# Turning normalized tokens by transfers and 32x32 blocks on VectorE in place of TensorE transposes, in a linear-attention and two-MLP kernel

## The chip, the cores and the metric

One core of one Trainium2 chip runs the whole program. Times are device microseconds of that core. The kernel before was timed three times: 986.84 to 987.23 us, median 987.09. Engines are named as in the profile: PE is TensorE's matmuls, PEld its weight loads, DVE is VectorE, ACT ScalarE, POOL GpSimd, SP the engine that issues nearly all transfers.

## The reference

```python
def phi(x):                                   # x is q or k, (4, 8, 576, 64), times 64 ** -0.25
    h = einsum('bhsd,md->bhsm', x, omega) - sum(x * x, -1) / 2
    return exp(h - max(h, -1)) / sqrt(128)
num = einsum('bhsm,bhmd->bhsd', phi(q), einsum('bhsm,bhsd->bhmd', phi(k), v))
x = num / (einsum('bhsm,bhm->bhs', phi(q), sum(phi(k), 2)) + 1e-6)      # to (2304, 512)
xn = x / sqrt(mean(x * x, -1) + 1e-6) * rms_g
y = (silu(xn @ w_gate) * (xn @ w_val)) @ w_out                          # 512 -> 1536 -> 512
out = silu(y @ w_in) @ w_out2                                           # 512 -> 2048 -> 512
```

Everything is float32 but the weights of the two MLPs, which come in as 64-bit words and are turned into float32 pairs on the chip.

## The kernel before

The 2304 tokens are 18 tiles of 128: 16 main tiles (a batch, a half, one of two interleaved rows) and 2 tail tiles of two batches each. Four tiles make a block; the normalized tokens of block j lie feature-first in the SBUF tile xs[j], which the instruction order names xs_90 to xs_94 (xs_93 is block 3, the last four main tiles; xs_94 the two tail tiles). Each float32 operand of a large product is kept as a high and a low part, and a product is three passes of TensorE.

The program has two phases.

**Phase one, 0 to 192.4 us**, is attention, normalization, the preparation of the first weights and the first gate, value and output products of blocks 0 to 2. It is a list of small operations (class `Op`: engine, estimated length, what it waits for, buffers claimed and freed) that `run_order` emits in the order of the hand-written table `ORDER`; each engine works its own part of that table strictly in order, SP's transfers too. Products of blocks 0 to 2 (line 248, line 1037) stand between attention pieces in the table.

A token tile passes through these steps: numerators on TensorE (line 813); denominators, reciprocal and quotient on VectorE (lines 827, 830, 840) into `xt`; the square sum on ScalarE (`square`, line 878); the power -1/2 on GpSimd (`rstd`, lines 889 and 892); the scale on ScalarE (`scale_x`, line 908, in place in `xt`); then `flip_x` (line 917), four 128x128 transposes on TensorE into a PSUM buffer `b`; `x_hi` on ScalarE (line 926) and `x_lo` on VectorE (line 931) read that PSUM buffer and write the high and low part of xs[j]. `xt` has two buffers, each for the two tiles of a half batch, freed by the last flip; `b` has six.

```python
        def flip_x(o):
            st.pt = buf(ps_a, [P, KC, P], "b", o.slot["b"])
            for c in range(KC):
                nc.tensor.transpose(st.pt[:, c, :], st.x[:, c * P:(c + 1) * P], ident)
```

Other names in the rows: line 658 is the feature projection, line 788 the flip of the exponentials e (evacuated to qT at line 794), line 729 the kv product, lines 154 to 192 the decoding of weight words (raw, m) into high and low parts (w). Gate and value weights are loaded by line 144, one transfer of 128x4x256 words each, other weights by line 142; `rms_g` by line 1114 into g_sb.

**Phase two**, from 192.43 us, is `stream()`: the first sweep on blocks 3 and 4 (`g1_glu`, tiles g, line 248), then all further sweeps of both MLPs, with weight preparation between (`Prep.tick`).

## Time and profile before

| what | value |
|---|---|
| median of three runs | 987.09 us (986.84 to 987.23) |
| profiled execution, own time | 987.54 us |
| its span, first to last instruction | 985.8 us |
| granted TensorE clock, mean | 1.00 of full speed |
| busy us: PE, DVE, ACT, POOL | 979.3 (99%), 562.8 (57%), 400.9 (41%), 294.2 (30%) |
| start of the stream | 192.43 us |

The span is a little shorter than the execution's own time, since it runs from the first to the last instruction. Busy shares over the whole span average two phases of a different kind; the stages are read apart below. In the chain of waits a piece is what the end of the program hung on at that moment.

### The profile page before, as it was taken

The numbers are of one execution on the slowest core, as the hardware profiler recorded it, in microseconds if no ns is written. First come the engines' busy times: TensorE is split into PE (matmuls) and PEld (weight loads), VectorE is DVE, ScalarE is ACT, GpSimd is POOL, SyncE is SP. The second block draws the span as 40 slices with busy tenths as digits, with TensorE's granted clock in tenths as the row PEclk, the third lists the DMA queues.
The fourth block names the chain that finished last, engine by engine and source line by source line (L and its number), as shares of the span: only waits on it lengthen the run. The fifth ranks groups of instructions, "written<-read, shape, count | busy, mean of one in ns | idle before, by whom it ended". The sixth has DMA issues, their size and how long they took to land.

```text
span 985.8 us, 15373 instructions
## 1 busy us (share of the span) xinstructions
PE 979.3 (99%) x6010; PEld 835.4 (85%) x6010; DVE 562.8 (57%) x1168; ACT 400.9 (41%) x922; POOL 294.2 (30%) x308
## 2 busy tenths in 40 slices
PE   9999999999999999999999999999999999999998
PEld 8999988887888888888898888888888888888887
DVE  7998976668633265774234773614634634535633
ACT  6999977753311123341112334443222223222321
POOL 8888664245400022442001322402402312201200
PEclk9999999999999999999999999999999999999999
DMA  7646220123200012221000121201101201100023
GB/s 182 156 115 164 80 63 22 44 65 101 71 21 0 1 43 65 83 89 44 1 1 5 60 65 43 64 22 44 64 22 40 68 22 44 43 1 22 22 86 107
DMA packets 69112, 55.58 MB, mean 56 GB/s; under 512 B 26160, under 2 KB 63280, under 8 KB 69040
## 3 DMA queue, kind: packets, MB, share of 16 engines
q1 hardware_dynamic: 68768, 54.54, 19.0%
q8 instruction: 47, 0.77, 0.3%
q14 instruction: 25, 0.20, 0.1%
q10 hardware_dynamic: 272, 0.07, 0.0%
HBM read 49.87 MB, written 4.72 MB: 55 GB/s over the span
## 4 chain that ended last, share of the span: by engine, by line
PE 94%; DVE 2%; DMA 1%; ACT 1%; issue 0%; POOL 0%; SPq 0%; DVEq 0%
PE g L248 45%; PE y L335 20%; PE y L302 13%; PE b L658 5%; PE b L248 3%; PE b L813 2%; PE kv L729 2%; PE b L1037 2%; PE b L788 2%; PE b L629 2%; PE b L917 1%; DVE w L192 1%; DMA va<-in_v_dram 1%; DVE small L675 0%; DMA raw<-in_moe_w_out_dram 0%
## 5 line engine op out<-in xcount | busy, mean ns | idle before, releaser
L248 PE MATMUL g<-xs,w 128*128 128x512 f32 (+1 forms) x2256 | 469.4, 367 | 0.0
L248 PEld LDWEIGHTS g<-xs,w 128*128 128x128 f32 x2256 | 391.2, 188 | 71.7
L168 POOL TENSOR_TENSOR m<-m,raw 128x512 int32<-128x512 int32 x136 | 189.5, 1393 | 590.6 <-issue 422.3
L242 DVE TENSOR_TENSOR h<-s,h 128x512 fp32r<-128x512 f32 (+1 forms) x134 | 95.8, 715 | 186.2 <-ACT h L241 186.2
L335 PE MATMUL y<-w,h 128*128 128x512 f32 (+1 forms) x870 | 201.0, 388 | 0.0
L335 PEld LDWEIGHTS y<-w,h 128*128 128x128 f32 x870 | 162.2, 188 | 33.3
L241 ACT ACTIVATE h<-s 128x512 fp32r<-128x512 f32 (+1 forms) x134 | 78.7, 588 | 184.2 <-DVE s L271 162.2
L302 PE MATMUL y<-h,w 128*128 128x512 f32 (+1 forms) x648 | 135.6, 366 | 0.5 <-DVE w L192 0.5
L302 PEld LDWEIGHTS y<-h,w 128*128 128x128 f32 x648 | 112.1, 189 | 20.8 <-DVE w L192 0.9
L282 ACT ACTIVATE s<-g 128x512 f32<-128x512 f32 (+1 forms) x80 | 44.5, 556 | 172.1 <-PE g L248 166.9
L346 DVE TENSOR_TENSOR ya<-y,ya 128x512 f32<-128x512 f32 (+1 forms) x91 | 62.2, 684 | 58.0 <-PE y L335 56.7
L271 DVE TENSOR_TENSOR s<-s,g 128x512 f32<-128x512 f32 (+1 forms) x54 | 33.9, 627 | 85.6 <-PE g L248 83.2
L313 DVE TENSOR_TENSOR ya<-y,ya 128x512 f32<-128x512 f32 (+1 forms) x80 | 50.2, 635 | 54.1 <-PE y L302 53.9
L700 ACT ACTIVATE e<-b,nb 128x128 f32<-128x128 f32 x272 | 76.2, 427 | 3.3 <-DVE nb L688 3.1
L189 ACT ACTIVATE w<-m 128x512 fp32r<-128x512 f32 x68 | 43.1, 634 | 68.6 <-POOL m L168 68.1
L658 PE MATMUL b<-bd,hl 128*128 128x256 f32 x432 | 62.3, 289 | 0.6 <-DVE hl L646 0.5
L658 PEld LDWEIGHTS b<-bd,hl 128*128 128x128 f32 x432 | 54.2, 189 | 2.4 <-DVE hl L646 0.7
L192 DVE TENSOR_TENSOR w<-m,w 128x512 fp32r<-128x512 f32 x68 | 54.1, 795 | 2.2 <-ACT w L189 2.2
L675 DVE TENSOR_REDUCE small<-b 128x4 f32<-128x512 f32 x72 | 50.1, 695 | 8.7 <-PE b L658 6.1
L265 ACT ACTIVATE s<-g 128x512 f32<-128x512 f32 (+1 forms) x54 | 29.6, 548 | 58.2 <-PE g L248 58.1
L582 POOL TENSOR_TENSOR sq<-sq 128x256 f32<-128x256 f32 (+1 forms) x80 | 46.5, 589 | 3.2
L578 POOL TENSOR_TENSOR sq<-x 128x512 f32<-128x512 f32 (+1 forms) x40 | 39.5, 992 | 21.8 <-DVE ns L591 13.3
(72 smaller groups left out, 738.0 us busy)
## 6 DMA issues: line engine op xcount, KB each, us to landing
raw<-in_moe_w_out_dram SPq DMA_DIRECT2D x28, 512.0 KB, 3.5
raw<-in_moe_w_in_dram SPq DMA_DIRECT2D x16, 512.0 KB, 3.7
raw<-in_moe_w_gate_dram SPq DMA_DIRECT2D x12, 512.0 KB, 3.5
raw<-in_moe_w_val_dram SPq DMA_DIRECT2D x12, 512.0 KB, 3.5
x<-in_k_dram SPq DMA_DIRECT2D x16, 256.0 KB, 3.6
va<-in_v_dram SPq DMA_DIRECT2D x32, 128.0 KB, 4.2
x<-in_q_dram SPq DMA_DIRECT2D x16, 256.0 KB, 3.2
out_dram<-ya SPq DMA_DIRECT2D x15, 256.0 KB, 2.0
```

The source lines that it names most:

```text
L168: tt(out=mi, in0=mi, in1=(low if step == 5 else high).bitcast(I32), op=ALU.add)
L192: nc.vector.tensor_tensor(out=st.t[:, 1, :], in0=st.m.bitcast(F32), in1=st.t[:, 0, :].bitcast(F32), op=ALU.subtract)
L241: nc.scalar.activation(out=ht[:, 0, :], in_=s, func=AF.Copy)
L242: nc.vector.tensor_tensor(out=ht[:, 1, :], in0=s, in1=ht[:, 0, :].bitcast(F32), op=ALU.subtract)
L248: nc.tensor.matmul(out=ps, lhsT=w[:, a, cc * P:(cc + 1) * P], rhs=xs[j][:, c, cc, :], start=(n == 0), stop=(n == 3 * KC - 1),)
L302: nc.tensor.matmul(out=ps, lhsT=wt[1, "o", f][:, a, d * P:(d + 1) * P], rhs=hs[f][:, c, :], start=(n == 0), stop=(n == nn - 1),)
L313: nc.vector.tensor_tensor(out=y[:, d, :], in0=ps, in1=y[:, d, :], op=ALU.add)
L335: nc.tensor.matmul(out=ps, lhsT=hs[f][:, a, t * P:(t + 1) * P], rhs=wt[2, "p", f][:, c, d0:d1], start=(n == 0), stop=(n == nn - 1),)
L346: nc.vector.tensor_tensor(out=o[:, t, d0:d1], in0=ps, in1=o[:, t, d0:d1], op=ALU.add)
L658: nc.tensor.matmul(out=st.ps[r][:, 2 * j:2 * j + 2, :].rearrange("p h m -> p (h m)"), lhsT=st.hl[:, c, 2 * r + j, :], rhs=bd[:, a, :], sta ...
L675: nc.vector.tensor_reduce(out=st.mx[:, G * r:G * r + G], in_=st.ps[r], axis=AX.X, op=ALU.max)
L700: nc.scalar.activation(out=st.e[r][:, h, :], in_=st.ps[r][:, h, :], func=AF.Exp, bias=st.nb[:, G * r + h:G * r + h + 1],)
```

## The change

Lines of the changed kernel are named where they matter: the numerators are line 850 there, denominators 864, quotient 877 and 884, the square 915, the power 926 and 929, the scale 945, e's flip 826 and its evacuation 832, the output product 1084, its sum 1096, the gate and value product 256, weight loads 146 and 148.

- `flip_x` becomes `move_x`: four transfers issued by SP per tile (line 954), each from 128 features of all 128 tokens in `xt` into one group of 32 partitions of xs[j], where the high part will be; the issue waits for the scale.
- A new VectorE operation (line 964) turns that 128x512 tile in blocks of 32x32 back into `xt`, writing with a step of four elements.
- `x_hi` (line 972) and `x_lo` (line 977) read the turned `xt` in SBUF instead of PSUM. `xt` is freed by the last x_lo, and the x_lo of a pair are chained. [...]
- A partition of xs[j] now holds other features than before (feature 128a + 32c + d instead of 128c + p), so the rows of gate and value weights are loaded to fit: each of the 24 loads is four transfers of 32x4x256 words. `g_sb` too is loaded in four.
- The pad EDGE lies in the third early weight tile to be allocated rather than in the one with slot 2.
- The flip of e by transfers is written in as well, but no tile uses it (`BY_DMA` is empty).
- `ORDER` is written anew (1239 operations instead of 1221).

```diff
-        def flip_x(o):
-            st.pt = buf(ps_a, [P, KC, P], "b", o.slot["b"])
-            for c in range(KC):
-                nc.tensor.transpose(st.pt[:, c, :], st.x[:, c * P:(c + 1) * P], ident)
-
-        fl = Op(
-            "xf", "PE", 0.436, flip_x, [xn, getattr(xs_, "flip", None)], ["b"],
-            [(xs_.op, "xt")] if last else [],
+        def move_x(o):
+            blocked = xs[j][:, 0, :, o0:o0 + P].bitcast(F32)
+            for a in range(4):
+                nc.sync.dma_start(
+                    out=blocked[32 * a:32 * a + 32],
+                    in_=st.x[:, P * a:P * a + P],
+                )
+
+        fl = Op("xd", "SP", 2.1, move_x, [xn, getattr(xs_, "flip", None)], xfer=1.5)
+        xs_.flip = fl
+        turned = lambda: st.x.rearrange("p (c t) -> p c t", c=KC)
+        tp = Op(
+            "xT", "DVE", 0.6,
+            lambda o: nc.vector.transpose(
+                out=st.x.rearrange("p (c t b) -> p b c t", c=KC, b=4),
+                in_=xs[j][:, 0, :, o0:o0 + P].bitcast(F32).rearrange("p b (c d) -> p b c d", c=KC),
+            ),
+            [fl],
         )
         hi = Op(
             "x_hi", "ACT", 0.52,
-            lambda o: nc.scalar.activation(out=xs[j][:, 0, :, o0:o0 + P], in_=st.pt, func=AF.Copy),
-            [fl],
+            lambda o: nc.scalar.activation(out=xs[j][:, 0, :, o0:o0 + P], in_=turned(), func=AF.Copy),
+            [tp],
         )
         xslo[ti] = Op(
-            "x_lo", "DVE", 0.6,
+            "x_lo", "DVE", 0.61,
             lambda o: nc.vector.tensor_tensor(
-                out=xs[j][:, 1, :, o0:o0 + P], in0=st.pt,
+                out=xs[j][:, 1, :, o0:o0 + P], in0=turned(),
                 in1=xs[j][:, 0, :, o0:o0 + P].bitcast(F32), op=ALU.subtract,
             ),
-            [hi], free=[(fl, "b")],
+            [hi, getattr(xs_, "low", None)], free=[(xs_.op, "xt")] if last else [], port=True,
         )
...
+        if turned:
+            return [cols[P * a:P * a + P].rearrange("(c d) f -> d c f", c=KC) for a in range(4)]
...
+        if isinstance(ap, list):
+            for a, rows in enumerate(ap):
+                nc.sync.dma_start(out=raw[32 * a:32 * a + 32].rearrange("p c f w -> p c (f w)"), in_=rows)
...
+            for a in range(4):
+                nc.sync.dma_start(
+                    out=g_sb[32 * a:32 * a + 32], in_=rms_g[P * a:P * a + P].rearrange("(c d) -> d c", c=KC)
+                )
```

**TensorE ahead of the stream.** In the kernel before, from the last matmul row of the tail's numerators (b_3484; the tail's first numerators stand just above, the last main ones 23 rows earlier) on; two more output groups and the stream's `g<-xs_93` follow after the last row shown.

```order
L813 MATMUL b_3484<-kvs_2932,qT_3482 64x65
L917 MATMUL b_3495<-ident,xt_3070 128x128 x4
L917 MATMUL b_3507<-ident,xt_3070 128x128 x4
L917 MATMUL b_3513<-ident,xt_3300 128x128 x4
L1037 MATMUL b_3522<-h_3415,w_4_2954 128x512 x3
L917 MATMUL b_3527<-ident,xt_3300 128x128 x4
L1037 MATMUL b_3542<-h_3415,w_4_2954 128x512 x3
L1037 MATMUL b_3522<-h_3504,w_5_2961 128x512 x3
L1037 MATMUL b_3542<-h_3504,w_5_2961 128x512 x3
L1037 MATMUL b_3555<-h_3415,w_4_2954 128x512 x3
L1037 MATMUL b_3555<-h_3504,w_5_2961 128x512 x3
L917 MATMUL b_3566<-ident,xt_3519 128x128 x4
```

In the change, from the last main tile's numerators (b_3450, b_3468) on; after the last row one more group of six output matmuls, the tail's 16 numerator matmuls and then `g<-xs_93` follow.

```order
L850 MATMUL b_3450<-kvs_3168,qT_3434 64x65 x8
L850 MATMUL b_3468<-kvs_3168,qT_3427 64x65 x8
L826 MATMUL b_3478<-ident,e_3463 128x128 x4
L1084 MATMUL b_3495<-h_3381,w_4_2804 128x512 x3
L1084 MATMUL b_3499<-h_3381,w_4_2804 128x512 x3
L826 MATMUL b_3503<-ident,e_3282 128x128 x4
L1084 MATMUL b_3495<-h_3483,w_5_2997 128x512 x3
L1084 MATMUL b_3499<-h_3483,w_5_2997 128x512 x3
L1084 MATMUL b_3522<-h_3381,w_4_2804 128x512 x3
L1084 MATMUL b_3527<-h_3381,w_4_2804 128x512 x3
L1084 MATMUL b_3522<-h_3483,w_5_2997 128x512 x3
```

The five turns of line 917 are gone from here, the output products stand behind the main numerators, and the tail's numerators have moved behind these.

**ScalarE ahead of the stream**, in the change, from the evacuation of e's flip for the tail (qT_3508) on; the squares of the last pair of main tiles (xt_3383) stand just above. xt_3097 is the pair before, xt_3574 the last tail tile.

```order
L832 ACTIVATE qT_3508<-b_3503 128x512
L1096 ACTIVATE ya_97<-b_3495 128x512
L945 ACTIVATE xt_3383<-xt_3383,rstd_3491 128x512
L972 ACTIVATE xs_93<-xt_3097 128x4x128 x2
L832 ACTIVATE qT_3535<-b_3478 128x512
L1096 ACTIVATE ya_97<-b_3499 128x512
L945 ACTIVATE xt_3383<-xt_3383,rstd_3491 128x512
L197 ACTIVATE w_1_3576<-m_3357 128x512
L1096 ACTIVATE ya_97<-b_3527 128x512
L915 ACTIVATE xs_94,ss_3585<-xt_3574 128x4x128
L945 ACTIVATE xt_3574<-xt_3574,rstd_3586 128x512
L972 ACTIVATE xs_93<-xt_3383 128x4x128 x2
```

x_hi of the last pair (line 972, xs_93<-xt_3383) stands behind the square and the scale of the tail tile.

**SP ahead of the stream.** Before:

```order
L144 DMA raw_2888<-in_moe_w_gate_dram 128x4x256
L519 DMA x_2904<-in_q_dram 64x4x64 x2
L144 DMA raw_2934<-in_moe_w_gate_dram 128x4x256
L144 DMA raw_3266<-in_moe_w_val_dram 128x4x256
L144 DMA raw_3610<-in_moe_w_val_dram 128x4x256
L144 DMA raw_3652<-in_moe_w_gate_dram 128x4x256
L144 DMA raw_3724<-in_moe_w_val_dram 128x4x256
```

Of the change:

```order
L146 DMA raw_3057<-in_moe_w_gate_dram 32x4x256 x4
L528 DMA x_3113<-in_q_dram 64x4x64 x2
L954 DMA xs_92<-xt_2785 32x4x128 x8
L146 DMA raw_3261<-in_moe_w_val_dram 32x4x256 x4
L954 DMA xs_93<-xt_3097 32x4x128 x8
L954 DMA xs_93<-xt_3383 32x4x128 x8
L954 DMA xs_94<-xt_3574 32x4x128 x4
L146 DMA raw_3634<-in_moe_w_val_dram 32x4x256 x4
```

The moves of four main tiles and a tail tile (20 issues) now stand between the weight loads, and value loads of phase two stand behind them.

## Rows read from the trace of the kernel before

**Rows 1.** Windows by stage: length, busy us (instructions) of PE, PEld, DVE, ACT, POOL, clock, DMA, GB/s
```profile
10.00:50.00 40.00, 39.50 (x572) 37.17 (x569) 37.15 (x107) 38.72 (x127) 34.56 (x51) 1.00 0.66 165
50.00:123.00 73.00, 72.69 (x987) 67.63 (x987) 66.03 (x185) 70.54 (x214) 54.74 (x79) 1.00 0.47 121
123.00:177.00 54.00, 54.00 (x541) 46.83 (x540) 40.93 (x114) 41.22 (x107) 27.22 (x35) 1.00 0.16 49
177.00:192.40 15.40, 15.40 (x111) 12.93 (x110) 11.14 (x23) 12.66 (x29) 5.36 (x7) 1.00 0.12 35
```

**Rows 2.** Chain of waits, in order of time to 193 us: start, us, what
```profile
17.26 0.96 PE b L658 x6
...
49.19 0.50 SPq L526
...
106.14 0.87 PE b L917 x8
...
174.45 1.08 PE b L813 x32
...
183.49 1.08 PE b L813 x32
184.57 1.46 PE b L917 x12
...
191.04 1.39 PE b L1037 x6
192.43 0.70 PE g L248 x3
```

**Rows 3.** Groups of one form, 0 to 192.4 us: busy us, mean ns | idle before
```profile
L840 DVE TENSOR_TENSOR xt<-b,rd 128x256 f32<-128x256 f32 x32 | 13.0, 418 | 0.4
...
L931 DVE TENSOR_TENSOR xs<-b,xs 128x512 fp32r<-128x512 f32 x18 | 12.0, 682 | 2.6 <-ACT xs L926 2.6
L926 ACT ACTIVATE xs<-b 128x512 fp32r<-128x512 f32 x18 | 11.0, 636 | 2.4 <-PE b L917 2.2
...
L192 DVE TENSOR_TENSOR w<-m,w 128x512 fp32r<-128x512 f32 x9 | 6.9, 766 | 1.3 <-ACT w L189 1.3
...
L830 DVE RECIPROCAL rd<-rd 128x4 f32<-128x4 f32 x36 | 5.5, 169 | 0.4
```

**Rows 4.** Groups of one form on VectorE, whole span
```profile
L157 DVE TENSOR_SCALAR raw<-raw 128x512 uint32<-128x512 uint32 x68 | 31.5, 464 | 0.0
L160 DVE TENSOR_SCALAR m<-m 128x512 f32<-128x512 f32 x68 | 29.7, 436 | 0.0
```

**Rows 5.** DMA issues of all kinds: count, KB each, us to landing
```profile
raw<-in_moe_w_val_dram SPq DMA_DIRECT2D x12, 512.0 KB, 3.5
...
out_dram<-ya SPq DMA_DIRECT2D x15, 256.0 KB, 2.0
...
x<-in_q_dram SPq DMA_DIRECT2D x8, 64.0 KB, 2.4
```

**Rows 6.** Timeline from 179 to 184 us: start, us, engine, line
```profile
179.68 0.66 ACT L878 ACTIVATE xs<-xt 128x512 fp32r<-128x512 f32 x1
...
180.81 0.22 ACT L878 ACTIVATION_READ_ACCUMULATOR xs<-xt 128x1 f32 x1
...
181.12 0.19 POOL L889 TENSOR_SCALAR ss<-ss 128x2 f32<-128x2 f32 x1 [1.08 <-ACT xs L878]
...
181.39 0.69 POOL L892 TENSOR_TENSOR rstd<-ss,mhalf 128x2 f32<-128x2 f32 x1
...
182.64 1.32 ACT L908 ACTIVATE xt<-xt,rstd 128x512 f32<-128x512 f32 x2
...
183.49 0.37 SPq L144 DMA_DIRECT2D raw<-in_moe_w_gate_dram  x1
```

**Rows 7.** Timeline from 204 to 212 us, a value load and its first reading
```profile
204.61 0.37 SPq L144 DMA_DIRECT2D raw<-in_moe_w_val_dram  x1
...
211.25 1.42 DVE L154 TENSOR_SCALAR m<-raw 128x512 uint32<-128x512 uint32 x1
```

More of the change, by code (lines that the diff above doesn't have):

```diff
@@ L115, with wcols @@
     assert f == NF2
-    wt = {}
-    def wcols(w, f):
-        return w.bitcast(U32)[:, 2 * f * P:2 * (f + 1) * P].rearrange("(c p) f -> p c f", p=P)
+    wt, early = {}, []
+    def wcols(w, f, turned=False):
+        cols = w.bitcast(U32)[:, 2 * f * P:2 * (f + 1) * P]
+        if turned:
+            return [cols[P * a:P * a + P].rearrange("(c d) f -> d c f", c=KC) for a in range(4)]
+        return cols.rearrange("(c p) f -> p c f", p=P)
     def wrows(w, f):
@@ L126, in prep_list @@
         if kind == 1:
[L127 removed]
+            gv = [e for f in fs for e in (("g", f, wcols(w_gate, f, True)), ("v", f, wcols(w_val, f, True)))]
             if si == 0:
@@ L184, in w_high @@
         t = pool.tile(
-            [P, 2 * KC * P + (EDGE if pool is pools["w"][2] and slot == W_EARLY - 1 else 0)], F32R,
+            [P, 2 * KC * P + (EDGE if pool is pools["w"][2] and len(early) == W_EARLY - 1 else 0)], F32R,
             tag=f"w{side}_{slot}", name=f"w{side}_{slot}",
         )
+        if pool is pools["w"][2]:
+            early.append(slot)
         st.t = t[:, 0:2 * KC * P].rearrange("p (a n) -> p a n", a=2)
@@ L693, in add_unit @@
         res = f"et{g}" if kind == "kt" else "e"
+        base = count[0]
+        if kind[0] == "q":
+            count[0] += R
+        moved = lambda r: kind[0] == "q" and base + r in BY_DMA
         for r in range(R):
@@ L697, in exps @@
                 pool = kp if kind == "kt" else wk
-                st.e[r] = buf(pool, [P, G, M], res, o.slot[res])
+                blocks4 = moved(r)
+                st.e[r] = buf(pool, [P, 4, G, 32] if blocks4 else [P, G, M], res, o.slot[res])
                 for h in range(G):
+                    src = st.ps[r][:, h, :]
                     nc.scalar.activation(
-                        out=st.e[r][:, h, :], in_=st.ps[r][:, h, :], func=AF.Exp,
+                        out=st.e[r][:, :, h, :] if blocks4 else st.e[r][:, h, :],
+                        in_=src.rearrange("p (a f) -> p a f", a=4) if blocks4 else src, func=AF.Exp,
                         bias=st.nb[:, G * r + h:G * r + h + 1],
@@ L711, in add_unit @@
         else:
-            evs = [add_flip_e(st, r, exs[r]) for r in range(R)]
+            evs = [add_flip_e(st, r, exs[r], moved(r)) for r in range(R)]
             num = None
@@ L780, in add_kv, with add_flip_e, move, turn @@
             add_tail(b - 1, g, 1, tst, tex, vop, [(tex, f"et{g}"), (pad, f"vt{g}")])
-    def add_flip_e(st, r, ex):
+    def add_flip_e(st, r, ex, by_dma):
         pe = {}
+        if by_dma:
+            def move(o):
+                pe[0] = buf(wk, [P, G, P], "qT", o.slot["qT"])
+                for a in range(4):
+                    nc.sync.dma_start(
+                        out=pe[0][32 * a:32 * a + 32],
+                        in_=st.e[r][:, a].rearrange("p h f -> p (h f)"),
+                    )
+            def turn(o):
+                turned = st.e[r].rearrange("p a h f -> p (a h f)").rearrange("p (h t) -> p h t", h=G)
+                nc.vector.transpose(
+                    out=turned.rearrange("p h (t b) -> p b h t", b=4),
+                    in_=pe[0].rearrange("p b (h f) -> p b h f", h=G),
+                )
+                st.e[r] = turned
+            mv = Op("ed", "SP", 2.1, move, [ex], ["qT"], xfer=1.5)
+            tp = Op("eT", "DVE", 0.6, turn, [mv], free=[(mv, "qT")])
+            return tp, (ex, "e")
         def flip(o):
@@ L815, in numerators @@
                     )
-        deps = evs + [prev, kvcopy[b, g]]
-        free = [(ev, "qT")]
+        deps = [ev for ev, _ in evs] + [prev, kvcopy[b, g]]
+        free = [evs[half_unit][1]]
         if tail:
@@ L945, in load @@
             w_load(job, st, o.slot["raw"])
-        lop = Op("ld_w", "SP", 0.5, load, gate, ["raw"], xfer=2.2)
+        lop = Op("ld_w", "SP", 2.1 if scaled(job) else 0.5, load, gate, ["raw"], xfer=2.2)
         prev = head = None
@@ L1113, with load_g @@
         bd_ops += spare
-        g_op = Op("ld_g", "SP", 0.5, lambda o: nc.sync.dma_start(out=g_sb, in_=rms_g.rearrange("(c p) -> p c", p=P)))
+        def load_g(o):
+            for a in range(4):
+                nc.sync.dma_start(
+                    out=g_sb[32 * a:32 * a + 32], in_=rms_g[P * a:P * a + P].rearrange("(c d) -> d c", c=KC)
+                )
+        g_op = Op("ld_g", "SP", 2.0, load_g)
         for u in units:
```

11 lines of the change are left out of this document (6 added, 5 removed), and 139 rows, old and new, of the table ORDER.

## The prediction

> **What bounds the kernel now.** I read the page first, whose busy times stand in the table above: TensorE is busy 99% of the span, so a change pays by what it takes off TensorE, or costs by a wait that it puts there. The windows by stage show where the change acts [rows 1]. From 10 to 192.4 us TensorE is busy 39.50 of 40, 72.69 of 73, 54.00 of 54 and 15.40 of 15.4 us. Beside it, up to 123 us, ScalarE is busy 38.72 + 70.54 = 109.3 of 113 us and VectorE 37.15 + 66.03 = 103.2: the reader is to see that three engines are nearly full there, and that after 123 us the two others have room (40.93 and 41.22 of 54). The chain of waits [rows 2] runs in TensorE pieces from 17.26 us to the stream, whose first matmul starts at 192.43 us; the turns of line 917 are in it at their full length, 0.87 us for two groups of four. The kernel's grouped instructions [rows 3] give the neighbours' prices.
>
> **What is removed.** 18 groups of four transposes leave TensorE. A group costs 0.87 / 2 = 0.44 us [rows 2], so 18 x 0.44 = 7.9 us leave a bound engine. That much is sure; what matters is what becomes of it.
>
> **What is added on VectorE.** Per token tile one turn of 128x512 from SBUF to SBUF, in 32x32 blocks. The trace has no such operation. The fast end is 0.44 us, what a one-input VectorE pass over 128x512 takes (line 160, [rows 4]); the slow end is twice an ordinary pass, 2 x 0.68 = 1.36. I take 0.68, a pass with two inputs over 128x512 (line 931, [rows 3]): of the two kinds of pass in these rows it is the one that goes slower per element, and a turn has to reorder what it reads. [...] x_lo now reads two SBUF tiles rather than PSUM; the like of that, line 192, takes 0.77 instead of 0.68 [rows 3], so 0.09 more. Per tile 0.77 us, for 18 tiles 13.9 us.
>
> From 10 to 123 us the kernel before has ten of the 18 groups (in the chain the last two of them start at 106.14 us, [rows 2]), and the new order still has the first eight turns there. TensorE's work falls by 10 x 0.44 = 4.4 us, so the stretch could shrink from 113 to 108.6. But ScalarE keeps its 109.3, and VectorE needs 103.2 + 8 x 0.77 = 109.4: both more than 108.6. So at least 0.8 us of the gain is not to be had, unless work of these two moves behind 123 us (then 0). Two engines with no idle time left will not mesh perfectly; I take **1.5 us**, with 0 and 4 as ends (4 is nearly all of the 4.4). Behind 123 us VectorE had 54 - 40.93 = 13 us idle; there the turns are covered.
>
> **What is added on the queue.** Four issues of SP per tile. One costs 0.37 us (line 144, [rows 6]) to 0.50 (line 526, [rows 2]); I take 0.44, so 1.8 us per tile. A load of 64 KB, the size of the four moves together, lands after 2.4 us, and the quickest transfer here after 2.0 [rows 5]; I take 2.2. A tile therefore passes from scaled to turned in 1.8 + 2.2 + 0.68 = 4.7 us, where TensorE needed 0.44. In the middle of the phase TensorE has other units' projections and products to do meanwhile, so this is hidden. Loads that stand behind a move on SP wait for that tile's scale; they are issued several units ahead, so I price them at nothing (if the cover fails, it shows as TensorE waiting on a DMA, inside the 4 us above).
>
> **Where the latency comes out: the start of the stream.** In the kernel before 16.9 us of TensorE work stood between the last main tile's numerators, which end at 174.45 + 1.08 = 175.53, and the stream [rows 2]. In the new order only this does: two flips of e (2 x 0.44), 24 output matmuls (4 x 1.39) and the tail's numerators (1.08) [rows 2], together 7.5 us. The stream's first group needs all four tiles of block 3, high and low part. From the end of the last main numerators the way is:
> - VectorE, two times denominator, reciprocal (0.17 each) and quotient (0.42): 1.5 us, some of it overlapped with the numerators, 1.2 [rows 3];
> - ScalarE, two squares, from 179.68 to 181.03 us: 1.3; GpSimd, rstd, from 181.12 to the end of the power at 182.08: 1.0; ScalarE, the scale of tile 0, half of 1.32: 0.7 [rows 6]. That is 4.2;
> - ScalarE then does two x_hi of the earlier tiles, one qT and one ya before it scales tile 1: 4 x 0.62 + 0.66 = 3.1, 7.3;
> - SP 1.8, landing 2.2, turn 0.7, in all 4.7: 12.0; x_hi 0.64 and x_lo 0.77 [rows 3]: 13.4;
> - seven handings-over between engines, 0.09 us each at best (as from 181.03 to 181.12, [rows 6]): 14.0 us.
>
> TensorE has 7.5 us of work for these 14.0, so **it waits 6.5 us** with nothing else in its queue (5 if landing and issue take their lower prices and one overlaps, 8.5 if the issues take 0.5 and the tail's square and scale, which stand before x_hi of these tiles on ScalarE, come last). The last tile of block 4 is later still, but it is wanted 48 matmuls x 0.23 (1.39 / 6, [rows 2]) = 11 us after the stream starts, and is covered.
>
> **Edits at nothing.** 24 gate and value loads become four issues each, 3 x 0.37 to 3 x 0.5 = 1.1 to 1.5 us later: the load issued at 204.61 lands after 3.5 us and is first read at 211.25, 3.1 us of room [rows 5, 7]. The three more issues for g_sb stand ahead of other loads near the start, 3 x 0.37 = 1.1 us; the loads of values that follow are issued well ahead of their use, and I take nothing, with 1.1 us as the other end if a first use falls due there. The weight tile moved is an address.
>
> **Sum.** -7.9 + 1.5 + 6.5 = +0.1 us. The profiled execution took 987.54 us, the median of the runs is 987.09, 0.45 less; so 987.54 + 0.1 - 0.45 = **987.2 us**: the gain on TensorE is spent at the start of the stream. A measurement of this kernel can tell 0.2%, 2.0 us, from no change.
>
> **Rivals.**
> 1. *The latency is hidden and the gain stays.* If the way to the stream takes some 10 us rather than 14 (moves that land while the next is issued, both tiles in parallel) the wait is 2.5, and with 1.0 for the middle the sum is -4.4: 982.7. With no wait at all -7.9 + 0.8: 980.0. For it: the first tile's move is in flight while the second tile is still being scaled, and the prices are taken one after the other. Against it: from the quotient to x_lo of the second tile each step hangs on the one before, and 7.5 us is all the work that TensorE has.
> 2. *VectorE becomes the bound, slower.* The turn writes its elements 16 bytes apart. If that halves the rate, a turn takes 1.36 us; the eight early ones then cost 8 x 0.68 = 5.4 us more on an engine that has no idle time left, and the last one 0.7 in the way to the stream: 987.2 + 6.1 = 993.3. It decides from 0.9 us per turn on: (0.9 - 0.68) x 9 = 2.0 us, 0.2%. Against it: a VectorE pass with 8-byte steps (line 157) takes 464 ns where the dense one (line 160) takes 436 [rows 4], 6% more; no row has 16-byte steps. [...]
> 3. *The change does less than it says.* Excluded: the instruction order has no turn of token tiles on TensorE any more.
>
> **How the numbers follow.** Forecast 0.45: with the middle at 0.8 to 3 and the wait at 5 to 7.5 the sum is -2.1 to +2.6, so 985.0 to 989.7; with the far ends of both (0 and 5, 4 and 8.5) it would be 984.2 to 991.7. Rival 1 0.29 (979.5 to 985). Rival 2 0.22 (989.5 to 994). 0.04 is left for what I don't see. The range 981.0 to 991.0 takes in the forecast, most of rival 1 and the lower part of rival 2. Faster than 985.1: rival 1 and a little of the forecast, 0.32. Slower than 989.1: rival 2, the forecast's top and the rest, 0.29. Within: 0.39.
>
> **What would show it.** Right: a wait of TensorE of 5 to 8 us in one piece ahead of the first stream matmul, released by x_lo (line 977) or x_hi; turns of 0.6 to 0.8 us; moves landing in 2.0 to 2.4 us; 0 to 4 us of short waits on VectorE or ScalarE between 50 and 123 us; a stream that starts within 2 us of 192.4. Wrong: a stream that starts near 186 (rival 1), or turns over 0.9 us and many waits on VectorE (rival 2).

## The result, and the profile after

| what | before | after |
|---|---|---|
| median of the runs (four each, same chip) | 987.16 us (986.84 to 987.52) | 996.92 us (996.45 to 996.95) |
| span of the profiled execution | 985.8 us | 995.2 us |
| start of the stream | 192.43 us | 201.3 us |
| from there to the end of the span | 793.4 us | 793.9 us |
| busy us: PE, DVE, ACT, POOL | 979.3, 562.8, 400.9, 294.2 | 977.5, 582.9, 402.1, 295.2 |

The ratio is 1.0098, with a 95% interval of 1.008 to 1.0115. The change makes the kernel slower by 9.8 us, where 0.1 us was forecast and 991.0 was the top of the range. Of the span's 9.4 us, 8.9 come before the stream starts.

The windows of after, with the stretches of [rows 1] and three more around the new start:

```profile
10.00:50.00 40.00, 38.70 (x552) 35.44 (x550) 36.88 (x102) 37.48 (x123) 34.53 (x53) 1.00 0.74 169
50.00:123.00 73.00, 70.11 (x919) 63.23 (x920) 69.14 (x187) 68.68 (x205) 54.46 (x77) 1.00 0.52 137
123.00:177.00 54.00, 51.62 (x488) 43.88 (x487) 49.56 (x115) 41.39 (x112) 26.31 (x33) 0.97 0.30 80
177.00:192.40 15.40, 15.40 (x134) 12.68 (x133) 11.15 (x28) 9.80 (x25) 6.85 (x8) 1.00 0.11 31
192.40:201.30 8.90, 3.53 (x43) 2.71 (x41) 5.98 (x14) 6.54 (x14) 1.14 (x3) 0.82 0.23 67
201.30:206.00 4.70, 4.70 (x13) 3.46 (x14) 2.32 (x3) 1.62 (x3) 0.00 (x0) 0.62 0.71 176
206.00:212.00 6.00, 6.00 (x28) 4.96 (x27) 2.46 (x6) 2.31 (x4) 0.00 (x0) 1.00 0.35 70
```

TensorE had 0.5, 0.3, 0 and 0 us idle in the first four [rows 1]; now it has 1.3, 2.9, 2.4 and 0, and 5.4 in the fifth. VectorE's busy time rose from 66.03 to 69.14 in the second window and from 40.93 to 49.56 in the third. The granted clock is below 1.00 in three windows, at 0.62 in the one after the start of the stream; it was 1.00 in all stretches before.

The waits of TensorE in after (engine, line, what it waited for: us in total, times, longest):

```profile
PE g L256 <- DMA xs<-xt: 5.4, 1, 5.4
PE b L1084 <- DVE h L1060: 1.8, 1, 1.8
PE b L850 <- DVE hl L656: 1.5, 2, 0.8
...
PE b L668 <- ACT e L716: 1.0, 2, 0.8
PE b L826 <- ACT e L716: 0.8, 2, 0.6
...
PE b L850 <- DVE s L1051: 0.5, 1, 0.5
```

In before the only waits of 0.5 us or more in phase one were 1.4 us at the very start (there still) and one of 0.5 us. The first row is the wait that was forecast; the others, of 1.8 us at most, are new and on VectorE and ScalarE.

Groups of one form of after, 0 to 201.3 us (busy us, mean ns | idle before), and the issues of the moves (count, KB, us to landing):

```profile
L964 DVE STREAM_TRANSPOSE xt<-xs 128x512 f32<-128x512 f32 x17 | 18.7, 1110 | 1.2 <-DMA xs<-xt 1.1
...
L977 DVE TENSOR_TENSOR xs<-xt,xs 128x512 fp32r<-128x512 f32 x17 | 13.9, 825 | 0.9 <-ACT xs L972 0.9
...
L160 DVE TENSOR_SCALAR m<-raw 128x512 uint32<-128x512 uint32 x9 | 7.4, 825 | 0.0
L200 DVE TENSOR_TENSOR w<-m,w 128x512 fp32r<-128x512 f32 x9 | 6.1, 682 | 0.0
L163 DVE TENSOR_SCALAR raw<-raw 128x512 uint32<-128x512 uint32 x9 | 5.9, 661 | 0.0
```

```profile
xs<-xt SPq DMA_DIRECT2D x72, 64.0 KB, 2.2
```

A turn takes 1.11 us and x_lo 0.83 [before: rows 3, line 931]. The first two decode passes of a weight tile, lines 160 and 163 now, were lines 154 and 157; the rows show them at 0.83 and 0.66 us, and before they took 0.45 and 0.49:

```profile
L157 DVE TENSOR_SCALAR raw<-raw 128x512 uint32<-128x512 uint32 x9 | 4.3, 493 | 0.0
...
L154 DVE TENSOR_SCALAR m<-raw 128x512 uint32<-128x512 uint32 x9 | 4.0, 452 | 0.0
```

**Where 9.4 us of span come from.** The flips took 7.9 us off TensorE and the wait before the stream put 5.4 on. The stream starts 201.3 - 192.43 = 8.9 later, so the rest of phase one cost 8.9 + 7.9 - 5.4 = **11.4 us**, where 1.5 was forecast. The windows of that whole stretch, before and after, part it in two:

```profile
10.00:192.43 182.43, 181.63 (x2204) 164.59 (x2202) 155.27 (x426) 163.14 (x474) 121.88 (x171) 1.00 0.39 102
10.00:201.30 191.30, 179.35 (x2128) 157.94 (x2126) 172.71 (x442) 163.90 (x474) 123.29 (x171) 0.98 0.46 116
```

TensorE is idle for 191.30 - 179.35 - 5.4 = 6.6 us outside the wait, against 0.8 before: 5.8 us are new idle time. The other 5.6 are busy time: it should have fallen to 181.63 - 7.9 = 173.7 and is 179.35 for the same matmuls. Of this the clock of 0.94 in the 27 us from 150 to 177 (shown with fix150) makes 0.06 x 27 = 1.6; the rest is spread over the phase and was not traced to its places. In phase two, nearly cancelling things add up to +0.5. The first 48 matmuls of the stream take 13.03 us in the timeline (11.06 before): 2.0 lost, at the clock of 0.62. And many pieces of later gate and value products are 0.08 us shorter; one in the chain of waits of before, and its like in after:

```profile
245.51 16.40 PE g L248 x72
```

```profile
256.47 16.32 PE g L256 x72
```

After 300 us, before had six pieces of 8.24 and six of 8.16 us for 36 such matmuls; after has eleven of 8.16 and one of 8.19. With the other lengths it is 18 or 19 pieces times 0.08, about 1.5 us gained.

### The profile page after: what moved, and what is told of

It is laid out like the page before. It is cut to its first block, busy times and chain, and to the rows that moved or that the text cites. A ratio compares the mean times of both kernels' runs of the same rounds, so it can differ in the third digit from the quotient of the medians.

```text
span 995.2 us, 15601 instructions
## 1 busy us (share of the span) xinstructions
PE 977.5 (98%) x5938; PEld 830.0 (83%) x5938; DVE 582.9 (59%) x1186; ACT 402.1 (40%) x922; POOL 295.2 (30%) x308
## 4 chain that ended last, share of the span: by engine, by line
PE 86%; DVE 7%; ACT 2%; DMA 1%; issue 1%; POOL 1%; SPq 0%; DVEq 0%; ACTq 0%; POOLq 0%
PE g L256 44%; PE y L343 20%; PE y L310 12%; PE b L256 2%; PE b L668 2%; PE b L1084 2%; DVE small L685 1%; PE b L850 1%; ACT e L716 1%; PE kv L746 1%; PE b L639 1%; PE b L826 1%; DVE w L200 1%; DVE m L160 1%; DVE raw L163 1%
## 5 line engine op out<-in xcount | busy, mean ns | idle before, releaser
L592 POOL TENSOR_TENSOR sq<-sq 128x256 f32<-128x256 f32 (+2 forms) x80 | 46.7, 595 | 2.7
```

## Experiments on the turn

Times are medians; before took 986.9 to 987.2 us beside each of them. "Stream" is the start of the first product of block 3, "40 to 70" the busy time of an engine in that stretch of 30 us. Before and after have there, with the columns of [rows 1]:

```profile
40.00:70.00 30.00, 29.86 (x467) 28.08 (x467) 28.14 (x82) 29.72 (x94) 23.59 (x41) 1.00 0.41 100
```

```profile
40.00:70.00 30.00, 26.91 (x373) 24.04 (x373) 29.50 (x78) 28.33 (x86) 22.75 (x33) 1.00 0.57 143
```

**Each turn done twice** (label twice).

```diff
-            lambda o: nc.vector.transpose(
+            lambda o: [nc.vector.transpose(
...
-            ),
+            ) for _ in range(2)],
```

> Every turn is done twice (the second gives the same result): 18 x 1.1 us more on VectorE, nothing else. Theory A (VectorE is the bound up to about 123 us and partly after): the time rises by 10 to 17 us, to 1007 to 1014. Rival C (the loads behind the moves set the pace): it rises by 2 to 5 us, mostly the one turn in the way to the stream.

Measured 1011.51 us (1009.99 to 1011.71), 14.6 more than after, for 18 x 1.11 = 20 us more of VectorE, inside theory A's 10 to 17; the stream started at 214.5. So most of what is put on VectorE in this phase comes out in the time.

**Turns left out** (noturn) and **turns written densely** (dense): in the second the elements of a turn stand side by side, and the final stores put the tokens right again.

```diff
-                out=st.x.rearrange("p (c t b) -> p b c t", c=KC, b=4),
+                out=st.x.rearrange("p (c b t) -> p b c t", c=KC, b=4),
```

```diff
-            lambda o: nc.vector.transpose(
...
+            lambda o: None,
```

> The turns on VectorE are left out (so the products run on tokens that were not turned); moves, x_hi, x_lo and all else stay. Theory A: the middle gets back nearly all of the 11.4 us that TensorE falls behind there, and one turn less stands before the stream: 985 to 989. Rival C: 1 to 3 us less than the change, 994 to 996.

> The turn writes its result densely (the tokens of a tile come out in another order, which the last stores undo); everything else stays. Theory A (the 16-byte step of the turn's output costs the second half of its 1.11 us, and VectorE is the bound between 43 and 102 us): a turn takes 0.55 to 0.70 us, some 13 turns of the middle give back 0.4 us each, the time falls by 5 to 7 us to 990 to 992. Rival B (a turn of float32 takes 1.1 us whatever the step): turn and time stay, 996 to 998. Rival C (the middle loses its time to loads that stand behind the moves on SP): the turn gets faster, the time falls by less than 2 us.

Measured 994.16 us (991.74 to 995.07) without turns: only 2.8 gained, so the turns explain the smaller part of the loss and theory A fails. The time is rival C's, but not for its reason, as the run without moves below shows. Measured 1009.04 us (1008.01 to 1010.3) with dense turns, outside all three ranges. The turn itself became what the rival of the prediction needed (group of the turn, whole span):

```profile
L971 DVE STREAM_TRANSPOSE xt<-xs 128x512 f32<-128x512 f32 x18 | 12.6, 704 | 3.9 <-DMA xs<-xt 3.8
```

0.70 us dense against 1.11 with the step of 16 bytes, and the stream started at 199.3, 2.0 earlier; but the program ended 12 us later. TensorE's last matmul ended at 989.9 and the span at 1007.6, 17.7 us behind it (3.4 in after). Whether the stores did that, a second run had to tell: **dense_plain** has the dense turn and plain stores, on top of the two edits of the run both (below).

> As the run with the two edits together, with the turn written densely (no 16-byte step), and the results stored plainly, so that the tokens of a tile stand in another order in the output. Theory: a turn takes 0.70 instead of 1.11 us; 8 early ones give back about 2 us of the middle and the last one 0.4 us: 988.0 to 989.0 us, still above the kernel before, and phase two takes 793.5 to 794 us, so that the 14 us that the run with the dense turn lost at its end belong to its stores. Rival: if the dense turn is slow in phase two for another reason than the stores, the program stays near 1003 us.

Measured 990.13 us (989.53 to 991.07), against 991.21 for both. Phase two took 792.6 us, so the loss at the end of dense belonged to its stores in permuted order. The dense turn is worth 1.1 us there, half or less of what was expected.

## Experiments on the wait before the stream

**No moves and no turns** (nomove), and **blocks 3 and 4 turned on TensorE**, at the places of their moves (pe_tail).

```diff
-            for a in range(4):
-                nc.sync.dma_start(
...
+            pass
...
-            lambda o: nc.vector.transpose(
...
+            lambda o: None,
```

> Moves and turns are left out (x_hi reads the scaled, unturned tile); x_lo, weight loads and the order stay. Theory A2 (in the middle the loss lies in the new order on VectorE and ScalarE, which are full there, not in the moves on SP): the middle stays as without turns, only the wait before the stream falls by issue and landing, from 4.6 us to about 0.5, and with it the slow matmuls behind it: 987 to 990. Rival S (the moves on SP hold up loads and so the middle): it gains 3 us and more in the middle too, 980 to 986.

```diff
+        def flip_x(o):
...
+        on_pe = j >= 3
-        fl = Op("xd", "SP", 2.1, move_x, [xn, getattr(xs_, "flip", None)], xfer=1.5)
+        fl = (
+            Op("xf", "PE", 0.436, flip_x, [xn, getattr(xs_, "flip", None)], ["b"])
+            if on_pe else Op("xd", "SP", 2.1, move_x, [xn, getattr(xs_, "flip", None)], xfer=1.5)
+        )
...
```

In this edit and in pe_all below an operation whose inputs or buffers are not there yet also stands back until they are, so the order of the table is not kept throughout.

> The tiles of blocks 3 and 4 are turned on TensorE again, at the places where their moves stood; the other tiles are moved and turned as in the change (the features of those two blocks come in an order that their weights don't have). Theory A2: six flips cost 2.6 us, the wait of 5.4 us before the stream goes, and so does the slow stretch behind it; the middle stays: 992 to 995. Rival T (the wait before the stream is not from the moves but from the chain of squares and scales): the wait stays above 3 us, 996 to 1000.

Measured 994.28 us (992.87 to 994.55) and 997.94 us (996.4 to 998.64). The waits of TensorE in the first, and in the second:

```profile
PE g L256 <- ACT xs L964: 4.6, 1, 4.6
```

```profile
PE b L980 <- ACT xt L963: 3.0, 1, 3.0
```

Without moves and turns the wait is still 4.6 us: x_hi of the last pair is queued on ScalarE behind the tail tile's square and scale. With TensorE flips it is 3.0 us, released by the scale of the tail, whose flip stands ahead of the stream in TensorE's queue there. Two ways of nearly equal length lead to the stream, and neither edit takes away both. So theory A2 fails in both runs, and rival T holds in pe_tail.

The run without moves says more. Its time is that of the run without turns (994.16), so the moves and what stands behind them on SP cost little, against rival S and rival C. And its stream starts at 197.88: with neither a move nor a turn, the rest of phase one still cost 197.88 - 192.43 + 7.9 - 4.6 = 8.8 us of the 11.4. What it keeps of the change is above all x_lo from SBUF (0.85 us instead of 0.68 per tile) and the new order.

**All tiles turned on TensorE in the new order** (pe_all, `on_pe = True` in the edit above, weights in the old layout) were to show the order alone:

> All tiles are turned on TensorE in the new order, at the places where their moves stood; no moves, no turns on VectorE, x_lo from PSUM; weights and g_sb still load in four pieces, in the old layout. Theory A2 (the new order itself loses 3 to 5 us, by VectorE operations held up in 150 to 165 us): 990 to 993. Rival V (the order is as good as the old one; moves, turns and x_lo from SBUF make the whole loss): 986 to 988.5.

It took 1017.85 us (1015.3 to 1020.2) and tells nothing of the order alone: TensorE waited in some fifteen places for qT, e and the low parts of features to be written. Likely the flips at the moves' places claim PSUM buffers that this order doesn't have free; that was not tried. So no run shows the new order by itself.

**Spare matmuls in the wait** (warm): 36 matmuls of 256 columns into an unused PSUM buffer, behind the tail's numerators.

```diff
+            if tail:
+                tails.append(1)
+            if tail and len(tails) == 4:
+                spare_ps = buf(ps_a, [P, G, D + 1], "kv", 0)
+                for _ in range(36):
+                    nc.tensor.matmul(
+                        out=spare_ps.rearrange("p g d -> p (g d)")[:, 0:G * D], lhsT=xs[2][:, 0, 0, 0:P], rhs=xs[2][:, 0, 0, 0:G * D],
+                        start=True, stop=True,
+                    )
```

> 36 matmuls of 256 columns into a PSUM buffer that is free by then stand in TensorE's queue behind the tail's numerators, where it waits for the stream's tokens; nothing else. Theory K (the first 4.7 us of the stream run at a granted clock of 0.62 because TensorE was idle before): these are granted 1.0, the time falls by 1 to 2 us, to 995 to 996. Rival (the slow stretch is hidden behind later waits): 996.5 to 997.5.

Measured 994.41 us (993.03 to 994.88), 2.5 gained, a little more than theory K's 1 to 2. The windows of warm, with the columns of [rows 1]:

```profile
195.00:201.30 6.30, 5.20 (x34) 4.42 (x34) 3.65 (x6) 2.79 (x6) 0.74 (x2) 1.00 0.27 79
195.00:206.00 11.00, 9.90 (x55) 8.31 (x55) 6.11 (x8) 5.31 (x9) 0.74 (x2) 1.00 0.49 133
```

The clock stays at 1.00 where after had 0.82 and 0.62. The wait of 5.4 us thus cost its own length and 2.0 to 2.5 us of slow matmuls behind it.

**The second scale of the last pair moved up** (both_scale, on top of both), directly behind the first on ScalarE:

```diff
-        969, 1233, 907, 1236, 902, 1111, 903, 908, 1012, 1234, 970, 1237, 904, 909, 994, 995, 996,
-        1232, 974, 1013, ...
+        969, 974, 1233, 907, 1236, 902, 1111, 903, 908, 1012, 1234, 970, 1237, 904, 909, 994, 995,
+        996, 1232, 1013, ...
```

> As in the run before, and the scale of the last pair's second tile stands directly behind that of the first on ScalarE (before: two x_hi, an evacuation of e's flip and one of an output product between them). Theory T (the way of the last pair through scale, move, turn and split sets the wait): that scale starts about 1.9 us earlier and the stream 1.0 to 1.9 us earlier, 989.0 to 989.9 us. Rival U (SP's twelve issues, 0.6 to 0.8 us each, set it): the second tile's moves are issued no earlier than SP has done the first's, so 0.3 us at most, 990.6 us.

Measured 991.48 us (991.25 to 991.74), against 991.21 for both: no gain. The scales now stand together, the second 1.8 us earlier (at 188.45 instead of 190.28), and SP's row of twelve issues for the last pair and the tail tile takes the same 9.26 us. The timeline of both_scale (in both the issues run from 188.41 on, also for 9.26 us), and below it eight issues of after that stand close together:

```profile
187.84 1.33 ACT L954 ACTIVATE xt<-xt,rstd 128x512 f32<-128x512 f32 x2
188.58 9.26 SPq L963 DMA_DIRECT2D xs<-xt  x12
...
194.61 0.72 ACT L954 ACTIVATE xt<-xt,rstd 128x512 f32<-128x512 f32 x1 [0.94 <-POOL rstd L938]
```

```profile
155.66 5.17 SPq L954 DMA_DIRECT2D xs<-xt  x8
```

An issue takes 5.17 / 8 = 0.65 us, where the prediction took 0.44. The eight of the last pair take 5.1 us in both runs; the rest of the 9.26 is SP waiting for the tail's scale (194.61) and its four issues. In both_scale the second tile's scale was done at 189.2, but its first issue came at 191.2, when SP was through with the first tile's four. So SP's issues hold the way through the moves, as rival U said; the time is 0.9 us over the one that it named.

## Experiments on the middle

**x_lo left out** (nolo), **x_hi left out** (nohi), **x_hi and turns left out** (nohi_noturn).

```diff
-            lambda o: nc.scalar.activation(out=xs[j][:, 0, :, o0:o0 + P], in_=turned(), func=AF.Copy),
+            lambda o: None,
...
-            lambda o: nc.vector.tensor_tensor(
-                out=xs[j][:, 1, :, o0:o0 + P], in0=turned(),
...
+            lambda o: None,
```

> x_lo is left out for all tiles (the low parts of the tokens are what lay there before); moves, turns and all else stay. Theory A2 (VectorE's extra load is only a few us of the loss, since ScalarE is full beside it): 993 to 996. [...]

> x_hi is left out on ScalarE (the high part is then what the move put there, unturned); moves, turns, x_lo and the order stay. Theory A3 (between 45 and 110 us ScalarE and VectorE are both full and each by itself holds the pace, so that taking from one gives little): a little more than without the turns, 990 to 994. Rival V (VectorE alone holds the pace): 995 to 997. Rival S (ScalarE alone): 987 to 990.

> x_hi and the turns are left out together. Theory A3: the middle up to 110 us gets back its 3 us and more, more than the two single gains add up to; the stall near 160 us and the wait before the stream stay: 985 to 989. Rival O (the middle's loss is set by the order of TensorE's own queue, whatever the others do): as without turns alone, 993 to 995.

Measured 992.25 us (992.07 to 994.06), 996.33 (994.94 to 996.74) and 992.36 (991.65 to 993.71): 4.7, 0.6 and 4.6 gained. The first is 0.75 us under the range of theory A2, the last lies between the two ranges named for it; the second is rival V's. Taking work off VectorE helps, off ScalarE alone hardly. But even the last kept 28.02 us of TensorE in 40 to 70, 1.8 short of before, with VectorE still busy for 28.68. Something else filled VectorE.

What it was shows in the timeline of after where the 1.8 us wait for h arises (start, us, engine, line):

```profile
158.81 3.02 POOL L174 TENSOR_TENSOR m<-m,raw 128x512 int32<-128x512 int32 x2 [3.81 <-DVE rd L864]
...
159.29 1.38 DVE L1060 TENSOR_TENSOR h<-s,h 128x512 fp32r<-128x512 f32 x1 [0.48 <-ACT h L1057]
...
160.59 1.53 DVE L160 TENSOR_SCALAR m<-raw 128x512 uint32<-128x512 uint32 x1
...
161.91 1.10 POOL L177 TENSOR_TENSOR m<-m,g_sb 128x512 f32<-128x512 f32 x1
162.04 1.52 DVE L1060 TENSOR_TENSOR h<-s,h 128x512 fp32r<-128x512 f32 x1
...
163.62 0.95 PE L1084 MATMUL b<-h,w 128*128 128x512 f32 x2 [1.82 <-DVE h L1060]
```

Three VectorE passes that take 0.67, 0.42 and 0.67 us at their shortest (lines 1060 and 160) take 1.38, 1.53 and 1.52 while GpSimd adds words for a weight tile and multiplies it by g_sb (line 177). The second and the third end 0.3 and 0.55 us behind the end of a GpSimd pass (161.83 and 163.01). TensorE waits for the third.

**Three decode steps moved** behind the two low parts of h (fix150):

```diff
-        ... 864, 1118, 1119, 1160, 1161, ... 886, 1093, 946, 925, 1188, 867,
+        ... 864, 1160, 1161, ... 886, 946, 925, 1188, 1118, 1119, 1093, 867,
```

> One place of the order changed: three decoding steps of VectorE stand behind two h_lo instead of ahead and between, so that GpSimd's two integer additions (3 us, at 157 us) start behind these. Theory A3 (VectorE's steps that are held up while GpSimd adds cost TensorE 3.7 us there, in its wait for h and in the slow matmuls behind it): 993 to 994.5. Rival W (the delay only moves to the next wait): 996 to 997.

Measured 993.43 us (992.66 to 994.16), 3.5 gained by three entries of the table, as theory A3 gave. The wait is gone. The stretch of 150 to 177 us in after, and in fix150:

```profile
150.00:177.00 27.00, 25.18 (x182) 20.55 (x181) 23.70 (x52) 20.51 (x52) 9.88 (x14) 0.94 0.17 46
```

```profile
150.00:177.00 27.00, 26.90 (x221) 22.13 (x221) 22.17 (x57) 22.71 (x57) 12.34 (x16) 1.00 0.18 52
```

So the gain is the wait of 1.8 us and the 1.6 that the clock cost there.

**GpSimd's weight passes left out** (noadds).

```diff
...
-                "w_add", "Pool", 1.28, lambda o, s=s: w_decode(job, st, s), [prev, g_op],
+                "w_add", "Pool", 1.28, lambda o: None, [prev, g_op],
```

> Left out: GpSimd's three passes per weight tile (lines 174 and 177) in phase one, with the last shift of VectorE's decode set to zero places, so the weights of the first sweep are other numbers; VectorE's passes stay as many as they were. Theory H (VectorE is held up while GpSimd reads SBUF, and this is the rest of the loss in the middle): the decode passes of lines 160 to 171 between 10 and 70 us come down from 0.52 to 0.85 us each to about 0.44, 3 to 4 us in all; TensorE's busy time between 40 and 70 us rises from 26.9 to 29 or more, and the program takes 992 to 994 us. Rival O (the order itself: VectorE and ScalarE work that is due too early, whatever each pass takes): the decode passes may be shorter, but TensorE's busy time there stays below 28 us and the program takes 995.5 us or more.

Measured 992.88 us (992.12 to 993.73). The time is what theory H gave, but not for its reason: TensorE had 27.25 us in 40 to 70, and the decode passes there stayed long. The gain came later, between 123 and 177 us:

```profile
123.00:150.00 27.00, 26.90 (x284) 23.75 (x285) 25.88 (x65) 21.67 (x64) 10.13 (x14) 1.00 0.42 109
150.00:177.00 27.00, 27.00 (x224) 22.48 (x223) 22.70 (x61) 21.95 (x55) 4.56 (x10) 1.00 0.20 55
```

Theory H falls for 40 to 70 us. What stands beside the long passes there are other GpSimd passes, the squares of q and k (timeline of after):

```profile
45.64 1.04 POOL L588 TENSOR_TENSOR sq<-x 128x512 f32<-128x512 f32 x1 [0.65 <-DVE ns L601]
...
46.15 0.82 DVE L160 TENSOR_SCALAR m<-raw 128x512 uint32<-128x512 uint32 x1
46.76 2.08 POOL L592 TENSOR_TENSOR sq<-sq 128x256 f32<-128x256 f32 x3
46.89 0.97 DVE L163 TENSOR_SCALAR raw<-raw 128x512 uint32<-128x512 uint32 x1
```

**The squares left out** (nosq), also **with the turns** (nosq_noturn), and **two of five decode passes left out** (nodec, on top of noadds).

```diff
-            nc.gpsimd.tensor_tensor(out=w.sq, in0=xf, in1=xf, op=ALU.mult)
+            nc.gpsimd.memset(w.sq.rearrange("p (a d) -> p a d", d=D)[:, :, 0:D // 4], 1.0)
...
-            nc.gpsimd.tensor_tensor(
...
+            pass
```

```diff
...
-                "w_dec", "DVE", 0.37, lambda o, s=s: w_decode(job, st, s, o.slot.get("wm")), [lop, prev],
+                "w_dec", "DVE", 0.37, lambda o, s=s: None if s % 2 else w_decode(job, st, s + s // 4 * 4, o.slot.get("wm")), [lop, prev],
```

> Left out: GpSimd's squares of q and k and their halvings (lines 588 to 594); a short memset stands in their place, so the norms of the features are a constant. In the run without GpSimd's weight passes the decode passes between 40 and 70 us kept their 0.8 to 1.3 us, and what GpSimd had beside them there were these squares. Theory H2 (VectorE is held up by the squares, and is full): the decode passes of lines 160 to 171 between 40 and 70 us come down to 0.42 to 0.5 us, VectorE gets some 2 us back there, TensorE's busy time in the stretch rises from 26.9 to 28.5 or more, and the program takes 993.5 to 995 us. Rival O (order): the passes get shorter, but TensorE's time in the stretch stays below 27.6 us and the program takes 996 us or more.

> The squares left out as in the run before, and the turns too. Theory H2: both are VectorE time in a stretch where VectorE is full (2.3 us of turns, some 2 us of hold-ups), so together they give back the whole loss between 40 and 70 us: TensorE busy 29.3 us or more of 30 there, and the program takes 990 to 992 us. Rival O: TensorE stays at or below 28.3 us there (27.2 with the turns alone left out) and the program takes 993.5 us or more, about as without the turns alone (994.2).

> Left out in phase one: two of VectorE's five decode passes per weight tile (lines 163 and 168), beside GpSimd's three weight passes as in the run that left those out alone (992.9 us, TensorE 27.25 us busy between 40 and 70 us). Theory H2 (VectorE is full there): 2.7 us of VectorE work leave the stretch, so TensorE's busy time there rises to 28.7 or more and the program takes 990.5 to 991.7 us. Rival O: below 27.8 us, and 992.3 us or more.

The same two passes in nosq:

```profile
45.69 0.42 DVE L160 TENSOR_SCALAR m<-raw 128x512 uint32<-128x512 uint32 x1
46.02 0.42 DVE L163 TENSOR_SCALAR raw<-raw 128x512 uint32<-128x512 uint32 x1
```

All nine decode passes between 40 and 70 us are back at 0.42. The stretch in nosq, and in nosq_noturn:

```profile
40.00:70.00 30.00, 28.10 (x387) 25.55 (x385) 28.51 (x87) 29.79 (x92) 5.71 (x16) 1.00 0.58 149
```

```profile
40.00:70.00 30.00, 28.24 (x391) 25.68 (x389) 27.13 (x83) 29.87 (x92) 6.21 (x18) 1.00 0.59 149
```

nosq took 993.21 us (991.93 to 994.09), 3.7 less than after, with the stream at 198.38; TensorE got 1.2 us back in the stretch, less than the 1.6 that H2 asked for and more than its rival allowed. nosq_noturn took 992.47 us (990.53 to 993.08) and got no further in the stretch: VectorE has room now (27.13), and ScalarE is busy for 29.87 of 30. So VectorE held the stretch first, and ScalarE is likely next; H2 holds for 1.2 of the 3 us. That ScalarE is next was not tried: x_hi was left out only with the squares still there (nohi_noturn, 28.02). nodec took 990.87 us (990.66 to 991.74), as H2 gave, but with 27.99 us of TensorE in the stretch, under H2's 28.7: its further gain came elsewhere.

**Two edits together** (both): the three decode steps of fix150 and the matmuls of warm.

> Two edits together: three decode steps placed behind the two low parts of h (alone: 3.5 us gained), and 36 spare matmuls in the wait before the stream (alone: 2.5 us). If the two losses are separate they add: 996.9 - 6.0 = 990.9 us, with a stream start near 198.5 us and no clock below 1.00 between 150 and 212 us. If the first edit only moved its gain into the tail wait, which the second then cannot fill, 993 us.

Measured 991.21 us (991.17 to 991.44), ratio 1.0039 with an interval of 1.0024 to 1.0054: 5.7 of the 6.0 us. The two losses are separate. It is the best version here that computes all of the reference, and still 4.2 us slower than the kernel before.

## Why the prediction was wrong, step by step

**The step that failed is "I take 1.5 us" for the middle, with 0 and 4 as ends, and with it "Behind 123 us ... the turns are covered".** The rest of phase one measured 11.4, and 3.5 of it lie behind 123 us (fix150). The reading that two engines beside TensorE were full was right. But the sum prices only the added passes, at fixed lengths, and has no term for what the new order does to all the others: without any move or turn 8.8 of the 11.4 stay (nomove). A misreading stands in it too: before has eight of the 18 groups of flips ahead of 123 us, not ten, so 8 x 0.44 = 3.5 us were to be had there instead of 4.4. The runs show these parts of the cost; they overlap and don't add exactly, and leaving a pass out also takes away the waits for its result.
- *Passes had no fixed length.* The busy times of VectorE were added up at mean prices. Line 160, from SBUF to SBUF, took 0.82 us beside GpSimd's squares (46.15) and 1.53 beside its additions (160.59), in place of 0.42. In the new order more of the first decode passes are long: 0.83 and 0.66 us on average for lines 160 and 163, against 0.45 and 0.49 before. Worth 3.7 us by nosq, which leaves the place near 160 us as it was (25.18 of 27), and 4.0 by noadds. The trace of before hinted at it: w's low part took 0.77 us on average against 0.68 for x_lo [rows 3], which I put down to its operands; in after it is the other way round, 0.68 for w's (line 200) and 0.83 for x_lo.
- *One place of the order.* Decode steps ahead of an urgent low part, beside two long GpSimd passes: 3.5 us by fix150. It is partly the first reason at one place, since noadds removes the same wait.
- *The turn's price.* 1.11 us, not 0.68. Rival 2 priced this (1.36, by 16-byte steps) and decides from 0.9; it was the right side. But at 0.43 us over the price, eight or nine turns give 3.4 to 3.9 us, and 987.2 + 3.9 = 991.1; leaving all turns out gives back 2.8, writing them densely 1.1. So rival 2 alone doesn't reach 996.9.
- *What stays open.* With VectorE relieved, ScalarE is busy for 29.87 of 30 us between 40 and 70 at 28.2 us of TensorE work, where before it was at 29.72 with 29.9. Why the new order has as much of ScalarE for less of TensorE there was not tried, and the new order was not run by itself.

**The wait before the stream: 6.5 forecast, 5.4 measured**, one piece, at its place, inside 5 to 8.5. Here the mechanism was right. The way in after:

```profile
187.14 1.15 PE L850 MATMUL b<-kvs,qT 128*64 128x65 f32 x32
...
194.57 0.72 ACT L945 ACTIVATE xt<-xt,rstd 128x512 f32<-128x512 f32 x1
...
199.49 1.09 DVE L964 STREAM_TRANSPOSE xt<-xs 128x512 f32<-128x512 f32 x1 [0.90 <-DMA xs<-xt]
...
200.62 0.63 ACT L972 ACTIVATE xs<-xt 128x512 fp32r<-128x512 f32 x1 [0.67 <-DVE xt L964]
...
201.30 5.08 PE L256 MATMUL g<-xs,w 128*128 128x512 f32 x13 [5.38 <-DMA xs<-xt]
```

Counted from the end of the main numerators (188.29), the second tile was scaled after 7.0 us (forecast 7.3), turned after 12.3 (12.0), and the stream began after 13.0 (14.0), 0.05 us behind the end of the last x_hi; TensorE had 7.6 us of work (7.5). That some terms cancelled is luck: an issue took 0.65 us instead of 0.44 and the turn 1.09 instead of 0.68, but a move lands 2.2 us after its issue begins, so that issuing and landing overlap, and the x_lo that the sum had in the way (0.77) is not waited for by the first matmul. A second way, over the tail's square and scale on ScalarE, is only 0.8 us shorter (4.6 in nomove); the prediction had it in its end of 8.5.

**What was not priced.** Behind the wait the granted clock was 0.62, with matmuls in the wait 1.00 (warm): 13.03 instead of 11.06 us for the stream's first 48 matmuls, 2.0 us. And "the weight tile moved is an address" was priced at nothing; pieces of the first MLP's products shortened by 0.08 us, about 1.5 us in all. That the moved tile did this is possible, since little else in phase two changed but the loads; it was not tried alone, and the cause stays open.

**What held.** The 18 groups of flips left TensorE, 7.9 us by their price; its busy time to the stream fell by 2.3 only, as the other matmuls took longer. The loads in four parts cost nothing, as no wait of TensorE on a weight transfer is new. x_lo at 0.77 was 0.83.

**Sum.** Forecast -7.9 + 1.5 + 6.5 = +0.1. Measured -7.9 + 11.4 + 5.4 + 2.0 - 1.5 = +9.4, the difference of the spans. The signs that the prediction named for rival 2, turns over 0.9 us and many waits on VectorE, are what came; the chance of 0.29 for slower was too low, and its range went to 994, 2.9 us short.

## What to carry to other kernels

Where three engines are full, the busy time of a pass in one place is no price for it in another (0.42 to 1.53 us here for line 160): look at the spread of same-shaped passes, and at what GpSimd does while the long ones run, before adding work to VectorE. An order written for an engine at its limit should be checked at the few places where an urgent pass stands behind an unhurried one; three entries moved were worth 3.5 of 9.8 us. A new order deserves a price of its own, and a run by itself. The wait of 5.4 us ahead of a long run of matmuls cost 2.0 to 2.5 us more than its length; with 36 spare matmuls in it the clock stayed at 1.00.

## What was unexpected of the hardware

- **VectorE beside GpSimd.** The same pass (line 160, in after) took 0.42 us with GpSimd idle (149.71), 0.82 beside its squares (46.15) and 1.53 beside its additions (160.59), and 0.42 each time between 40 and 70 us with the squares gone (nosq). Reductions kept their length: line 685 took 0.69 us (53.66) and line 601 0.28 (52.04) beside the squares in after, and 0.69 and 0.28 on average in nosq without them. The two passes at 160.59 and 162.04 ended 0.3 and 0.55 us behind the end of a GpSimd pass, less than the 0.42 and 0.67 that they take at their shortest. By what the one engine holds up the other no run shows.
- **A 16-byte step.** A turn of 128x512 took 1.11 us with it and 0.70 densely (dense), 0.41 us apart for 512 elements per partition. The row of 8-byte steps that the prediction set against it, 6% slower, did not foretell this: with the squares gone, passes with 8-byte steps (lines 160, 163, 168) and without (166, 171) all take 0.42 us, so that those 6% need not come from the step.
- **Issues of SP** took 0.65 us (5.17 for eight) for each move from SBUF to SBUF, against 0.37 and 0.50 for the loads of [rows 2, 6]. Single loads by line 528 took 0.66 too (at 67.22 and 120.02 us in after), so the length is not the moves' alone.
- **Stores in permuted order**: those of dense, main and tail tiles, in place of plain ones, left 17.7 us between TensorE's last matmul and the end, against 3.4 in after.
- **The granted clock** fell to 0.94 over 150 to 177 us, with a wait of 1.8 us in it, and to 0.62 in the 4.7 us behind the wait of 5.4. Without the first wait (fix150) and with matmuls in the second (warm) it was 1.00 in these stretches. But the profiled run of warm has the wait of 1.8 us too, and the clock was 1.00 from 150 to 177 us, so what decides it there stays open.
